# Attention and two feed-forward layers on one core: the stores of the first layer's converted weights in GpSimd's queue in place of SyncE's

## The chip, the cores and the metric

The kernel runs on one core of a Trainium2 chip. The metric is the device time of one execution in microseconds (us). The engines are named as in the profile: PE is TensorE (matmuls), DVE is VectorE, ACT is ScalarE, POOL is GpSimd, and SP is SyncE, which only issues transfers. A "q" behind an engine's name means its instruction queue. Transfers that an engine issues are carried out by the 16 DMA engines of the core.

## The reference

Attention over a band of keys and over block summaries of the keys, then two gated feed-forward layers; 1536 tokens (two batches of 768), 512 wide.

```python
def _attn_ref(q, k, v):                       # (2, 8, 768, 64) each
    k_sum = k.reshape(B, H, nb, 32, D).max(axis=3)
    v_sum = v.reshape(B, H, nb, 32, D).mean(axis=3)
    scores_l = scale * q @ k^T, kept where |i - j| < 16, else -1e9
    scores_s = scale * q @ k_sum^T + log(32)
    a = softmax(concat(scores_l, scores_s))
    return a @ concat(v, v_sum)

def _moe_ref(x, w_gate, w_val, w_out):        # 512 -> 1536 -> 512
    gate = 1.0 / (1.0 + np.exp(-(x @ w_gate)))
    val = x @ w_val
    return (gate * val @ w_out)

def _moe2_ref(x, w1, w2, w3, w_out):          # 512 -> 768 -> 512
    h = np.maximum(np.maximum(x @ w1, x @ w2), x @ w3)
    return (h @ w_out)
```

All inputs are float32. The weights reach the kernel as 64-bit numbers, so each weight tile has to be turned into float32 on the chip.

## The kernel before

**Stages.** Attention is cut into units of a batch, a pair of heads and half a sequence; units of batch 0 come first. As soon as batch 0 is attended, TensorE begins the first layer for it (`make_A`, gate and value products, L791; `make_B`, output products, L830), while the units of batch 1 run in between. From about 228 us on the first layer of batch 1 is computed with fewer, larger products (`make_Q`, L1023, and `make_B` again), then the second layer (`make_P`, L924) and its output (`make_D`, L1124). Each float32 matmul is made of three passes over a high and a low part of both operands, so that a weight tile "w" holds two parts.

**Converting a weight.** `convert` does this for 36 tiles of the first layer (24 of gate and value, "g" and "v", 12 of the output weights, "o", in three groups of 8 + 4). `to_float` loads a 512 KB tile "raw" (L409, SyncE; three buffers) and turns it into float32 in a 256 KB buffer "c" with three VectorE instructions, here called c1 (L416), c2 (L421) and c3 (L425). `split` then writes the high part of "w" on ScalarE (L358) and the low part on VectorE by a subtraction (L361); there are ten "w" buffers. There are only **two "c" buffers**: c1 of a tile can begin when the last but one tile has been split and, if it is a g or v tile, stored.

**Keeping it.** `keep` stores what batch 1 will need again in device memory, directly behind the conversion: a g or v tile is stored from "c" (256 KB, L457, into `kept_g` or `kept_v`), an o tile from "w" (512 KB, L451, into `kept_o`). That is 24 + 12 transfers, all between about 24 and 187 us. They are read back later (L480, L470) by SyncE.

**The order.** Nothing is scheduled on the chip. `Plan.order` sorts all tasks before the kernel is built: each task has an engine, a duration and a due time, and the planner keeps for each engine the time at which it is free, for transfers also a time of the queue. For a transfer of SyncE it reckons with 0.45 us to issue, 0.65 us until it begins and a duration that grows with its size. The instructions of every engine are written in the order that comes out, and each engine works through its own in that order, waiting where data or a buffer is missing. Changed durations in the planner so change the order on all engines. Attention's inputs "k", "q", "v", "vn" (L548), the raw loads and the stores all stand in SyncE's queue.

Of the kernel before, what the change touches and what calls it, by code (L numbers as in the profile page):

```python
# [31 lines left out]
KEEP, AGAIN = 4.0, 6.0  # L32
# [10 lines left out]
SLOW = 1.12  # L43
# [31 lines left out]
class Plan:  # L75
# [11 lines left out]
    def add(self, eng, dur, due, fn, deps=(), new=(), uses=(), after=(), tab=None):  # L87
        t = Task(eng, dur, due, fn, [d for d in deps if d], list(new), list(uses), [d for d in after if d], tab)
        self.tasks.append(t)
        return t  # L90
# [26 lines left out]
    def order(self):  # L117
        engs = ("PE", "DVE", "ACT", "POOL", "SP")
        free = dict.fromkeys(engs, 0.0)
        free["SP"] = 0.6  # L120
        dge = ring = 0.0
        clock = self.Clock()
        free["PE"] = 1.13
        tab = "E"
        taken = {}
        wait, then, ready = {}, {}, {e: [] for e in engs}
        for t in self.tasks:
            pre = t.deps + t.after
            wait[t] = len(pre)
            for d in pre:  # L130
                then.setdefault(d, []).append(t)
            if not pre:
                ready[t.eng].append(t)
        out = []

        def earliest(t):
            at = free[t.eng]
            for d in t.deps:
                at = max(at, d.end + self.lag(d, t) + (t.pad if d.eng != t.eng else 0.0))
            for d in t.after:  # L140
                at = max(at, d.start)
            need = {}
            for b in t.new:
                k = need.get(b.tag, 0)
                need[b.tag] = k + 1
                used = taken.setdefault(b.tag, [])
                i = len(used) + k - b.n
                if i >= 0:
                    for d in used[i].users:
                        if d.end is None:  # L150
                            return None
                        at = max(at, d.end + (0.1 if d.eng != t.eng else 0.0))
            return at

        def pressing(x):
            return x[1].due + (SWITCH if x[1].tab and x[1].tab != tab else 0.0)

        while len(out) < len(self.tasks):
            best = None
            for e in engs:  # L160
                c = [(at, t) for at, t in ((earliest(t), t) for t in ready[e]) if at is not None]
                if not c:
                    continue
                first = min(at for at, _ in c)
                at, t = min((x for x in c if x[0] <= first + SLACK[e]), key=pressing)
                if best is None or at < best[0]:
                    best = at, t
            at, t = best
            ready[t.eng].remove(t)
            t.start = at  # L170
            t.end = at + t.dur
            if t.eng == "PE":
                if t.new and at < FIRST + 5.0:
                    width = min(384, t.new[0].shape[-1] * (t.new[0].shape[1] if len(t.new[0].shape) == 3 else 1))
                    now = free["PE"]
                    while True:
                        end = clock.run(now, width / 2400.0, 1.0, False)
                        if end > at + OVER:
                            break
                        now = clock.run(now, width / 2400.0, 1.0) + 0.001  # L180
                        t.idle += 1
                    at = t.start = max(at, now)
                t.end = clock.run(at, t.dur, t.rows)
            if t.dma:
                dge = max(dge, at) + t.dma
                ring = max(ring, dge + 0.65) + (t.dur * SLOW if t.eng == "SP" else 0.2)
                free[t.eng] = at + t.dur if t.eng != "SP" else dge + 0.025
                t.end = ring
            if t.tab and t.tab != tab:
                tab = t.tab  # L190
                t.end += self.TABLE
            if not t.dma:
                free[t.eng] = t.end
            for b in t.new:
                taken[b.tag].append(b)
            out.append(t)
            for d in then.get(t, ()):
                wait[d] -= 1
                if not wait[d]:
                    ready[d.eng].append(d)  # L200
        return out
# [3 lines left out]
def kernel(  # L205
# [15 lines left out]
    nc = tc.nc  # L221
# [68 lines left out]
    add = plan.add  # L290
# [53 lines left out]
    at = FIRST  # L344
# [42 lines left out]
    def first_use(b, nm, f):  # L387
        if nm == "o" and b:
            return due["B", b, (f // GF, 0), 0, f % GF // 2] + 0.52 * (f % 2)
        if nm == "o":  # L390
            return due["B", b, (f // GF, 0), 0] + 0.52 * (f % GF)
        if nm == "l":
            return due["D", 0, 0, 0] + 0.68 * f
        return due[nm, b, f, 0]
# [3 lines left out]
    def convert():  # L398
# [3 lines left out]
        def to_float(ck, t):  # L402

            nonlocal n
            r = Buf(rp, [128, 2 * 512], I32, "raw", 3)
            c = Buf(cp, [128, 512], I32, "c", 2)

            def load(r=r, ck=ck):
                nc.sync.dma_start(out=r.t, in_=wts[row[ck[1:]]])  # L409

            def half(r, i):
                return r.t.rearrange("p (f two) -> p f two", two=2)[:, :, i]


            def c1(r=r, c=c):
                nc.vector.tensor_scalar(  # L416
                    out=c.t, in0=half(r, 1), scalar1=5, scalar2=2,
                    op0=ALU.logical_shift_left, op1=ALU.logical_shift_right)

            def c2(r=r, c=c):  # L420
                nc.vector.scalar_tensor_tensor(  # L421
                    out=c.t, in0=half(r, 1), scalar=-0x40000000, in1=c.t, op0=ALU.bitwise_and, op1=ALU.bitwise_or)

            def c3(r=r, c=c):
                nc.vector.scalar_tensor_tensor(  # L425
                    out=c.t, in0=half(r, 0), scalar=29, in1=c.t, op0=ALU.logical_shift_right, op1=ALU.bitwise_or)

            n += 1
            l = add("SP", 1.456, WFIRST + WSTEP * n if n <= 8 else t - WLOAD, load, new=[r], after=[prev.get("l")])
            k1 = add("DVE", 0.335, t - 2.7, c1, [l], [c], [r], [prev.get("1")])  # L430
            k2 = add("DVE", 0.602, t - 2.3, c2, [k1], [], [c, r])
            k3 = add("DVE", 0.602, t - 1.6, c3, [k2], [], [c, r])
            prev.update({"l": l, "1": k1})
            return c, k3
# [11 lines left out]
        def keep(ck, t, c, k):  # L446
            nm, f = ck[1:]
            if nm == "o":
                w, k = wt[ck], wready[ck]
                d = kept[nm, f] = Buf(kp, [128, 2, 512], F32, f"kept_o{f}", 1)  # L450
                d.k = add("SP", 1.456, t + KEEP, lambda: nc.sync.dma_start(  # L451
                    out=d.t, in_=w.t.bitcast(F32)), [k], [d], [w])
                return
            if f % 2 == 0:
                kept[nm, f // 2] = Buf(kp, [128, 2, 512], I32, f"kept_{nm}{f // 2}", 1)
            d = kept[nm, f // 2]
            k = add("SP", 0.73, t + KEEP, lambda: nc.sync.dma_start(out=d.t[:, f % 2], in_=c.t),  # L457
                    [k] + ([d.k] if f % 2 else []), [] if f % 2 else [d], [c] + ([d] if f % 2 else []))
            d.k = k

        for ck in chunks:
            t = first_use(*ck) - WREADY
            c, k = to_float(ck, t)
            wt[ck], wready[ck] = split(c, lambda c=c: c.t.bitcast(F32), t, [k])
            keep(ck, t, c, k)
# [9 lines left out]
        for g in range(NG):  # L475
            for nm, j in pairs[GF * g:GF * g + GF]:
                t = due["Q", nm, j, 1] - WREADY
                d = kept[nm, j]
# [9 lines left out]
        for nm, f, b in groups:  # L488
            if b == 0:
                t = due["P", nm, f, 0, 1] - WREADY  # L490
# [3 lines left out]
        for ck in last:  # L494
            t = first_use(*ck) - WREADY
            c, k = to_float(ck, t)
# [747 lines left out]
```

## Time and profile before

| | us |
|---|---|
| three runs, median (lowest to highest) | 551.56 (549.83 to 552.42) |
| the profiled execution | 553.78 |
| its span, first to last instruction | 552.0 |
| TensorE busy (matmuls) | 532.7 |
| VectorE busy | 418.5 |
| ScalarE busy | 305.0 |
| GpSimd busy | 3.7 |

TensorE is the engine with the most work, and it is busy for 96% of the span. The transfers of SyncE's queue take 40.3% of the time of 16 DMA engines, with most of it in the first third. A mean over the span says little here: the stages differ, and the stores that the change touches lie in the first 187 us alone. A row of a timeline gives the start, the duration, the engine, the line and the tile; in brackets stands how long the engine had been idle before it, and what ended that. A wait is put down to what came last. "issue" means that the profile shows nothing that was waited for.

### The profile page before, as it was taken

How to read it: one execution, taken by the hardware profiler on the slowest of the kernel's cores; microseconds unless marked ns; L12 is line 12 of the kernel's file. 1: busy time of each engine (PE TensorE's matmuls, PEld its weight loads, DVE VectorE, ACT ScalarE, POOL GpSimd, SP SyncE). 2: the span in 40 equal slices, each digit the busy share in tenths (PEclk: the TensorE clock that was granted, in tenths of full speed). 3: DMA queues.
4: the chain of work that ended last, by engine and by line, in shares of the span. 5: the costliest groups of instructions: out<-in, count | busy, mean ns of one | idle time of the engine just before them, and what ended most of it. 6: DMA issues, size and time to landing. Idle time of an engine off the chain costs nothing.

```text
span 552.0 us, 10064 instructions
## 1 busy us (share of the span) xinstructions
PE 532.7 (96%) x3805; PEld 506.0 (92%) x3805; DVE 418.5 (76%) x988; ACT 305.0 (55%) x722; POOL 3.7 (1%) x18
## 2 busy tenths in 40 slices
PE   7799999979979999999999999999999999999997
PEld 5688999969979999999999999998999999998886
DVE  3999997588788766998287589999999998995000
ACT  3879879578547785565465166544434343463111
POOL 2000000000000000000000000000000000000000
PEclk9999999999999999999999999999999999999999
DMA  8999897678866510143025028111322223201121
GB/s 270 292 309 319 293 350 222 225 250 290 275 167 185 214 50 2 38 148 121 28 93 173 14 77 300 43 39 43 112 76 78 77 78 113 77 2 39 57 76 58
DMA packets 28128, 78.25 MB, mean 142 GB/s; under 512 B 3504, under 2 KB 6960, under 8 KB 28080
## 3 DMA queue, kind: packets, MB, share of 16 engines
q1 hardware_dynamic: 24960, 73.87, 40.3%
q10 hardware_dynamic: 3120, 3.74, 1.9%
q8 instruction: 30, 0.49, 0.4%
q14 instruction: 18, 0.15, 0.1%
HBM read 61.28 MB, written 15.73 MB: 140 GB/s over the span
## 4 chain that ended last, share of the span: by engine, by line
PE 67%; DMA 13%; DVE 12%; ACT 4%; issue 1%; SPq 1%; ACTq 1%; DVEq 0%
PE m L830 13%; PE m L924 11%; PE s L924 10%; PE m L1124 9%; PE s L1023 8%; PE m L1023 8%; PE m L791 6%; DMA vn<-in_vn_dram 3%; DMA kept_g<-c 3%; DMA k<-in_kn_dram 2%; DMA kept_v<-c 2%; DVE w L361 2%; DVE c L425 2%; DVE c L421 2%; DVE e L661 1%
## 5 line engine op out<-in xcount | busy, mean ns | idle before, releaser
L791 PE MATMUL m<-x,w 128*128 128x384 f32 x576 | 109.6, 341 | 1.6 <-DVE t L813 1.3
L830 PE MATMUL m<-h,w 128*128 128x384 f32 x576 | 105.2, 336 | 0.0
L791 PEld LDWEIGHTS m<-x,w 128*128 128x128 f32 x576 | 98.6, 188 | 4.2 <-DVE t L813 1.6
L830 PEld LDWEIGHTS m<-h,w 128*128 128x128 f32 x576 | 99.6, 188 | 0.5 <-issue 0.3
L924 PE MATMUL m<-x,w 128*128 128x384 f32 x294 | 56.2, 334 | 0.6 <-ACT t L939 0.6
L924 PE MATMUL s<-f,w 128*128 128x384 f32 x294 | 56.0, 334 | 0.0
L358 ACT ACTIVATE w<-c 128x512 fp32r<-128x512 f32 (+1 forms) x60 | 35.5, 597 | 35.0 <-DVE c L425 28.4
L924 PEld LDWEIGHTS m<-x,w 128*128 128x128 f32 x294 | 51.4, 188 | 0.9 <-ACT t L939 0.9
L924 PEld LDWEIGHTS s<-f,w 128*128 128x128 f32 x294 | 51.4, 188 | 0.1
L667 ACT ACTIVATE e<-e,nm 128x120 f32<-128x120 f32 x96 | 36.7, 385 | 20.3 <-DVE nm L661 20.1
L1023 PE MATMUL s<-f,w 128*128 128x384 f32 x252 | 47.9, 335 | 0.0
L1023 PE MATMUL m<-f,w 128*128 128x384 f32 x252 | 46.7, 334 | 0.0
L1023 PEld LDWEIGHTS s<-f,w 128*128 128x128 f32 x252 | 43.9, 188 | 0.6 <-ACT t L1038 0.6
L1023 PEld LDWEIGHTS m<-f,w 128*128 128x128 f32 x252 | 43.9, 188 | 0.1
L421 DVE SCALAR_TENSOR_TENSOR c<-raw,c 128x512 int32<-128x512 int32 x60 | 41.1, 686 | 0.6
L425 DVE SCALAR_TENSOR_TENSOR c<-raw,c 128x512 int32<-128x512 int32 x60 | 41.1, 685 | 0.3
L361 DVE TENSOR_TENSOR w<-c,w 128x512 fp32r<-128x512 f32 (+1 forms) x60 | 38.6, 644 | 2.0 <-ACT w L358 2.0
L361 DVE TENSOR_TENSOR w<-raw,w 128x512 fp32r<-128x512 f32 (+1 forms) x48 | 28.2, 620 | 14.7 <-ACT w L358 14.6
L358 ACT ACTIVATE h<-t 128x384 fp32r<-128x384 f32 x48 | 24.9, 523 | 22.7 <-DVE t L1063 15.3
L416 DVE TENSOR_SCALAR c<-raw 128x512 int32<-128x512 int32 x60 | 25.2, 423 | 13.7 <-DMA kept_v<-c 9.7
L358 ACT ACTIVATE w<-raw 128x512 fp32r<-128x512 f32 (+1 forms) x48 | 25.8, 572 | 14.4 <-PE m L830 11.1
L361 DVE TENSOR_TENSOR h<-t,h 128x384 fp32r<-128x384 f32 x48 | 26.1, 553 | 7.3 <-ACT h L358 7.2
(128 smaller groups left out, 764.7 us busy)
## 6 DMA issues: line engine op xcount, KB each, us to landing
raw<-in_wts_dram SPq DMA_DIRECT2D x60, 512.0 KB, 4.5
kept_o<-w SPq DMA_DIRECT2D x12, 512.0 KB, 4.0
w<-kept_o SPq DMA_DIRECT2D x12, 512.0 KB, 6.5
k<-in_kn_dram SPq DMA_DIRECT2D x8, 400.0 KB, 6.4
q<-in_qt_dram SPq DMA_DIRECT2D x16, 192.0 KB, 5.5
v<-in_vw_dram SPq DMA_DIRECT2D x16, 192.0 KB, 5.1
kept_g<-c SPq DMA_DIRECT2D x12, 256.0 KB, 5.6
kept_v<-c SPq DMA_DIRECT2D x12, 256.0 KB, 4.5
```

The source lines that it names most:

```text
L358: nc.scalar.activation(out=dst, in_=src, func=ACTF.Copy)
L361: nc.vector.tensor_tensor(out=dst, in0=src, in1=h.bitcast(F32), op=ALU.subtract)
L416: nc.vector.tensor_scalar(out=c.t, in0=half(r, 1), scalar1=5, scalar2=2, op0=ALU.logical_shift_left, op1=ALU.logical_shift_right)
L421: nc.vector.scalar_tensor_tensor(out=c.t, in0=half(r, 1), scalar=-0x40000000, in1=c.t, op0=ALU.bitwise_and, op1=ALU.bitwise_or)
L425: nc.vector.scalar_tensor_tensor(out=c.t, in0=half(r, 0), scalar=29, in1=c.t, op0=ALU.logical_shift_right, op1=ALU.bitwise_or)
L661: nc.vector.tensor_tensor_reduce(out=e[h].t[:, t], in0=ps[h].t[:, t], in1=masks[:, var], scale=-SC, scalar=3.0e38, op0=ALU.add, op1=ALU.mi ...
L667: nc.scalar.activation(out=e[h].t[:, t], in_=e[h].t[:, t], func=ACTF.Exp, scale=-1.0, bias=nm.t[:, h, t:t + 1], accum_out=sm.t[:, h, t:t + 1])
L791: nc.tensor.matmul(ps.t, lhsT=w.t.rearrange("p s (k f) -> p s k f", k=KC)[:, wh, kc], rhs=src[kc // 2].t[:, xh, kc % 2], start=(kc == 0 an ...
L830: nc.tensor.matmul(ps.t, lhsT=w.t.rearrange("p s (k f) -> p s k f", k=KC)[:, wh, dm], rhs=h.t[:, xh], start=(i == 0 and j == 0), stop=(i = ...
L924: nc.tensor.matmul(ps.t, lhsT=w.t[:, wh, c:c + 128], rhs=x.t[:, xh, kc], start=new and n == 0, stop=n == 5, skip_group_check=True)
L1023: nc.tensor.matmul(ps.t, lhsT=w.t[:, wh, c:c + 128], rhs=x.t[:, xh, kc], start=new and n == 0, stop=n == 5, skip_group_check=True)
L1124: nc.tensor.matmul(ps.t[:, c0:c1], lhsT=h.t[:, xh, e, c:c + 128], rhs=w.t[:, wh, c0:c1], start=(f == 0 and i == 0), stop=(f == NF2 - 1 and ...
```

## The change

The stores of `keep` are issued by GpSimd, in its own queue, instead of SyncE. The planner gets figures for a transfer of GpSimd: the engine is taken for 1.0 us, the queue begins after 1.65 us, and the transfer ends 1.9 us and 2.2 times its duration after the issue. No instruction of another engine is added or removed; the order of the first 200 us or so changes on PE, DVE, ACT and SP.

```diff
@@ Plan.order
-            if t.dma:
+            if t.dma and t.eng == "POOL":
+                free["POOL"] = at + 1.0
+                ring = max(ring, at + 1.65) + t.dur * SLOW
+                t.end = at + 1.9 + 2.2 * t.dur
+            elif t.dma:
                 dge = max(dge, at) + t.dma
@@ keep
-                d.k = add("SP", 1.456, t + KEEP, lambda: nc.sync.dma_start(
+                d.k = add("POOL", 1.456, t + KEEP, lambda: nc.gpsimd.dma_start(
                     out=d.t, in_=w.t.bitcast(F32)), [k], [d], [w])
+                d.k.dma = 1.0
...
-            k = add("SP", 0.73, t + KEEP, lambda: nc.sync.dma_start(out=d.t[:, f % 2], in_=c.t),
+            k = add("POOL", 0.73, t + KEEP, lambda: nc.gpsimd.dma_start(out=d.t[:, f % 2], in_=c.t),
                     [k] + ([d.k] if f % 2 else []), [] if f % 2 else [d], [c] + ([d] if f % 2 else []))
+            k.dma = 1.0
```

Lines of the kernel after stand four (planner and conversions: L409 is L413, L416 is L420, L421 is L425, L425 is L429, L361 is L365) to six (L548 is L554) further down. In the rows below, the word ahead of "<-" is what is written, the one behind it what is read.

SyncE's queue before, where the second group of weights begins (83 to 96 us):

```order
L409 DMA raw<-in_wts_dram 128x1024
L457 DMA kept_v_1406<-c 128x512
L548 DMA q<-in_qt_dram 128x384
L548 DMA k<-in_kw_dram 128x720 x2
L409 DMA raw<-in_wts_dram 128x1024
L457 DMA kept_g_1360<-c 128x512
L548 DMA v<-in_vw_dram 64x768
L548 DMA v<-in_vw_dram 32x768
L409 DMA raw<-in_wts_dram 128x1024
L457 DMA kept_v_1406<-c 128x512
```

The same place of SyncE's queue after:

```order
L413 DMA raw<-in_wts_dram 128x1024
L554 DMA q<-in_qt_dram 128x384
L554 DMA k<-in_kw_dram 128x720 x2
L413 DMA raw<-in_wts_dram 128x1024 x2
L554 DMA v<-in_vw_dram 64x768
L554 DMA v<-in_vw_dram 32x768
```

and GpSimd's queue after, which holds nothing else there:

```order
L462 DMA kept_g_1331<-c 128x512
L462 DMA kept_v_1362<-c 128x512
L462 DMA kept_g_1331<-c 128x512
L462 DMA kept_v_1362<-c 128x512
L462 DMA kept_g_1546<-c 128x512
```

The stores are gone from between the loads, and each stands behind earlier stores alone.

VectorE before, inside the second group (from the c3 that ended at 102.44 us to the c1 of 112.06 and its c2):

```order
L425 SCALAR_TENSOR_TENSOR c<-raw,c 128x512
L416 TENSOR_SCALAR c<-raw 128x512
L361 TENSOR_TENSOR w<-c,w 128x512
L421 SCALAR_TENSOR_TENSOR c<-raw,c 128x512
L425 SCALAR_TENSOR_TENSOR c<-raw,c 128x512
L416 TENSOR_SCALAR c<-raw 128x512
L361 TENSOR_TENSOR w<-c,w 128x512
L421 SCALAR_TENSOR_TENSOR c<-raw,c 128x512
L425 SCALAR_TENSOR_TENSOR c<-raw,c 128x512
L416 TENSOR_SCALAR c<-raw 128x512
L421 SCALAR_TENSOR_TENSOR c<-raw,c 128x512
```

and VectorE after, one conversion later in the same group:

```order
L429 SCALAR_TENSOR_TENSOR c<-raw,c 128x512
L420 TENSOR_SCALAR c<-raw 128x512
L365 TENSOR_TENSOR w<-c,w 128x512
L425 SCALAR_TENSOR_TENSOR c<-raw,c 128x512
L429 SCALAR_TENSOR_TENSOR c<-raw,c 128x512
L365 TENSOR_TENSOR w<-c,w 128x512
L420 TENSOR_SCALAR c<-raw 128x512
L425 SCALAR_TENSOR_TENSOR c<-raw,c 128x512
L429 SCALAR_TENSOR_TENSOR c<-raw,c 128x512
L420 TENSOR_SCALAR c<-raw 128x512
```

In the first pair of conversions one more subtraction now stands between a c3 and the c1 after the next; otherwise the pattern is the same.

## Rows read from the trace of the kernel before

**Rows 1.** Stages: start:end, length, busy of each engine, PEclk, DMA share, GB/s.

```profile
25.00:50.00 25.00, 24.30 (x355) 22.18 (x354) 23.55 (x85) 21.65 (x76) 0.00 (x0) 1.00 0.95 328
50.00:100.00 50.00, 49.43 (x443) 46.41 (x442) 41.20 (x121) 43.20 (x111) 0.00 (x0) 1.00 0.89 287
100.00:125.00 25.00, 21.38 (x159) 19.19 (x159) 18.86 (x46) 16.04 (x39) 0.00 (x0) 1.00 0.66 216
150.00:175.00 25.00, 22.21 (x167) 20.54 (x166) 20.96 (x64) 13.61 (x47) 0.00 (x0) 1.00 0.64 188
228.00:350.00 122.00, 122.00 (x702) 121.28 (x701) 91.85 (x190) 67.76 (x139) 0.00 (x0) 1.00 0.32 113
```

**Rows 2.** Waits of TensorE, 30 to 230 us: total, times, longest; first two and last.

```profile
PE s L686 <- ACT e L681: 3.1, 2, 1.8
PE s L699 <- issue: 1.5, 1, 1.5
...
PE m L791 <- DVE x L361: 0.3, 1, 0.3
```

**Rows 3.** Timeline of TensorE: start, duration, line, tile; in brackets the idle time before.

```profile
114.96 2.36 PE L791 MATMUL m<-x,w 128*128 128x384 f32 x12 [1.26 <-DVE t L813]
...
119.09 0.90 PE L686 MATMUL s<-ident,e 128*120 128x128 f32 x3 [1.77 <-ACT e L681]
...
155.74 0.90 PE L686 MATMUL s<-ident,e 128*120 128x128 f32 x3 [1.29 <-ACT e L681]
```

**Rows 4.** Timeline of VectorE: two c3, then the c1 that waited.

```profile
90.78 0.69 DVE L425 SCALAR_TENSOR_TENSOR c<-raw,c 128x512 int32<-128x512 int32 x1
...
92.56 0.69 DVE L425 SCALAR_TENSOR_TENSOR c<-raw,c 128x512 int32<-128x512 int32 x1
...
100.09 0.43 DVE L416 TENSOR_SCALAR c<-raw 128x512 int32<-128x512 int32 x1 [2.26 <-issue]
...
104.56 0.43 DVE L416 TENSOR_SCALAR c<-raw 128x512 int32<-128x512 int32 x1 [2.12 <-DMA kept_v<-c]
...
112.06 0.43 DVE L416 TENSOR_SCALAR c<-raw 128x512 int32<-128x512 int32 x1 [2.42 <-DMA kept_v<-c]
...
149.10 0.43 DVE L416 TENSOR_SCALAR c<-raw 128x512 int32<-128x512 int32 x1 [2.44 <-DMA kept_v<-c]
```

**Rows 5.** Waits of VectorE, 0 to 200 us: total, times, longest.

```profile
DVE c L416 <- DMA kept_v<-c: 9.7, 5, 2.4
...
DVE k L636 <- DMA k<-in_kw_dram: 4.3, 4, 1.9
...
DVE c L416 <- issue: 2.3, 1, 2.3
...
DVE c L416 <- DMA kept_g<-c: 1.1, 1, 1.1
```

**Rows 6.** Timeline of SyncE's queue: start and duration of the issue.

```profile
93.77 0.42 SPq L457 DMA_DIRECT2D kept_g<-c  x1
...
95.96 0.50 SPq L457 DMA_DIRECT2D kept_v<-c  x1
...
106.95 0.33 SPq L409 DMA_DIRECT2D raw<-in_wts_dram  x1
107.33 0.42 SPq L457 DMA_DIRECT2D kept_v<-c  x1
```

**Rows 7.** Issue to landing: the 24 stores of L457; ScalarE's stores, KB each, median.

```profile
DMA to landing us min/median/max: 3.4/4.8/7.7
...
out_dram<-c ACTq DMA_DIRECT2D x11, 256.0 KB, 2.0
```

**Rows 8.** Timeline of GpSimd: a longest instruction, and its last one.

```profile
2.59 0.44 POOL L279 TENSOR_SCALAR_AFFINE_SELECT masks<-masks 64x288 f32<-64x288 f32 x1
...
4.75 0.11 POOL L286 MEMSET masks<- 64x16 f32 x1
```

**Rows 9.** Waits of SyncE's queue: total, times, longest.

```profile
SPq L409 <- DVE c L425: 150.7, 34, 23.1
```

## The prediction, made before the changed kernel ran

> **What bounds the kernel now.** I read the profile in this order: the table of stages, for the engine that sets the end; TensorE's waits and its timeline, for the places where that engine stands still; then VectorE's waits and its timeline, for what stands behind those places; and last SyncE's queue and the times to landing, because the change lies there. The stages [rows 1] show TensorE busy for 24.30 of 25 us from 25 us on, and for all of 122 us between 228 and 350. An engine that has work all the time ends when its work is done, so a change in front of it counts only as far as it fills a gap on TensorE or opens one. The gaps that can be filled lie in two stages: 25 − 21.38 = 3.62 us are idle between 100 and 125 us, and 25 − 22.21 = 2.79 us between 150 and 175 us [rows 1]. Over 30 to 230 us the waits of TensorE stand in 7 lines, from 3.1 down to 0.3 us, and sum to 7.7 us [rows 2]. This is all that a better order could win there, 1.4% of the time. A loss has no such limit.
>
> Three of the gaps can be followed back. The matmul group at 114.96 us waited 1.26 us for a VectorE product (L813); the transposes at 119.09 and 155.74 us waited 1.77 and 1.29 us for ScalarE's scaling (L681) [rows 3], which itself needs a VectorE reciprocal. VectorE, in order, stood a short time earlier at c1 (L416), the first step of a conversion, because c1 writes a buffer "c" of which there are only two, and the store of the last but one conversion had not landed: 2.26 us before 100.09, 2.12 before 104.56, 2.42 before 112.06, 2.44 before 149.10 [rows 4]. In the table of waits these are 9.7 us in 5 waits for kept_v, 1.1 in one for kept_g, and one of 2.3 put down to "issue", the one at 100.09 [rows 5]. Its predecessor by two is the store issued at 93.77, so I count it with them: 13.1 us in 7 waits. The stores that are to move are thus what VectorE waits for ahead of three of TensorE's gaps.
>
> **The change part by part.** *Leaving SyncE.* SyncE issues in order, and a store stands behind whatever is in front. The c3 (L425) that started at 90.78 us and took 0.69 ended at 91.47; its store left at 93.77, behind the kw loads and a raw load that the order has in front of it. The next c3 began at 92.56 [rows 4], ended at 93.25, and its store left at 95.96 [rows 6]. From the end of c3 to the c1 that needed the landing, these two took 100.09 − 91.47 = 8.6 us and 104.56 − 93.25 = 11.3 us. In the ordinary case only the raw load that c3 also releases stands ahead: raw at 106.95, store at 107.33 [rows 6], so 0.4 us after c3. With the median of 4.8 us to landing [rows 7] an ordinary store takes 0.4 + 4.8 = **5.2 us from c3's end**.
>
> *Going through GpSimd.* GpSimd has had nothing to do since its last instruction at 4.75 us [rows 8], so its 36 stores wait there for their data alone. The trace shows no transfer that GpSimd issued, so the price is bounded. From below: 2.0 us, a 256 KB store of ScalarE's queue with nothing ahead [rows 7]. From above: 7.7 us, the longest of the stores today [rows 7], if the work of GpSimd costs as much as the worst queue. I take the shortest of today's, 3.4 us [rows 7], which still has one 512 KB raw load in front of it, and add 0.44 us, GpSimd's longest instruction [rows 8]: **3.8 us from c3's end**. It lies nearer to the lower end because the row that is likest, a store behind one load, lies there. The saving is 5.2 − 3.8 = 1.4 us for each ordinary exposed store (bounds +3.2 and −2.5), and 8.6 − 3.8 and 11.3 − 3.8, more than their whole waits, for the two that SyncE held.
>
> *VectorE's waits.* Of the seven, 2.26 and 2.12 go. Of 2.42 and 2.44, 1.02 and 1.04 stay. The other two of kept_v's five are 9.7 − 2.12 − 2.42 − 2.44 = 2.7 us together, 1.4 each, and go, as the 1.1 of kept_g does. So 2.1 of 13.1 us stay.
>
> *TensorE's gaps.* Before 112.06 us VectorE gains 2.26 + 2.12 + 1.4 = 5.8 us, more than the 1.26 + 1.77 that TensorE loses at 114.96 and 119.09; by 149.10 it has gained more still, against 1.29. All three gaps go: **−4.3 us**. What is late next there is TensorE itself. The other 3.4 us of gaps, among them 1.5 of unseen cause [rows 2], stay.
>
> *The planner's new order.* The changed costs give another order up to about 200 us; behind that TensorE's order is the same. In the stretch of shortest cover (second group of weights) both orders put only a c1, one or two subtractions (L361) and c2, c3 between a store and the c1 that needs its buffer: 2.1 us before, 2.1 to 2.7 after. The order therefore hides no more of a store than it did, and part of the 2.1 us that stays on VectorE will be felt. Today 13.1 us of such waits cost 4.3 us on TensorE, 0.33 each; 2.1 × 0.33 = **+0.7 us**.
>
> *Costed at nothing.* SyncE's own freedom: it waits 150.7 us for c3 before raw loads [rows 9], because there are three raw buffers, so the loads come no sooner; VectorE waits for no raw load. Attention's loads no longer stand behind stores; VectorE waited 4.3 us for kw loads [rows 5], and what of that goes adds to 5.8 us that already exceed the gaps. Without that excess it would be worth up to 4.3 × 0.33 = 1.4 us. The 12 kept_o stores hold "w" buffers, of which there are ten, and VectorE and TensorE show no wait for one. The bytes are the same.
>
> Sum: −4.3 + 0.7 = −3.6 us. The profiled execution took 553.78 us, 1.78 more than its span of 552.0; it gives 550.2. The median of the three runs is 551.56, and on that scale the forecast is **548.0 us**, 0.65% less.
>
> **A rule that speaks against it.** In the rows the two stores that SyncE held left 2.3 and 2.7 us late, and that is where the first two waits begin. The Trainium skill, DMA: Bandwidth & Descriptors, section "Issuing engines are not separate DMA queues", says that transfers of all issuing engines end up on the same 16 DMA engines, and that issuing from several engines "will only save the time on the sequencer it takes to initiate the DMA". By that rule the sum would hold only the time lost ahead of the issue, and the trace shows that this is not small here; what it would make of the sum is the first rival.
>
> **The rivals.** *No change.* The store shares the DMA engines with the raw load of the same moment, and the DMA engines are 0.89 to 0.95 busy until 100 us [rows 1]; it lands at 5.2 us after c3 as today. Then only the two held stores gain. For it: landing, not issue, is most of the 5.2 us. Against it: from 100 us on the DMA share is 0.66 [rows 1], there is room. The attention units also go through ScalarE's exponentials, for which VectorE waits too; in this case the 1.77 and 1.29 stay, the 1.26 goes, and the new order returns 0.7: 551.56 − 1.26 + 0.7 = 551.0 us.
>
> *Slower: GpSimd and VectorE in each other's way.* What GpSimd must write for a transfer falls right behind c3, when VectorE is already in its next instructions, a c1 of 0.43 us among them [rows 4]. If the store then lands 7.7 us after c3, each of the seven waits grows by 2.5 us, 17.5 us on VectorE, at 0.33 on TensorE: +5.7, **557.3 us**. It decides against the change from 5.2 us on. For it: VectorE is 23.55 of 25 us busy in the first stage [rows 1]. Against it: a c1 is short beside 3.8 us. The Trainium skill, SBUF — State Buffer, section "SBUF: two separate sides", names such a mechanism: while VectorE runs an instruction in a mode that takes two ports, GpSimd cannot write the descriptors of its transfers. No run here shows it yet.
>
> *All gaps go.* Stores at 2.0 us, no VectorE wait left: 551.56 − 7.7 = 543.9 us.
>
> **How the numbers follow.** About 0.5% (2.8 us) is what a measurement here can tell from no change, so "faster" is below 548.8 and "slower" above 554.3. The forecast gets 0.46; its store lies between 2.0 and 5.2 us, and with it the time between 545 and 551, so that 0.34 falls below 548.8 and 0.12 above. All gaps gone: 0.10. No change: 0.22. Slower: 0.22. This makes faster 0.44, same 0.34, slower 0.22. The range begins at 544.0, the best that the gaps allow, and ends at 555.5, where the slower rival is at two thirds of its price; about 0.15 lie beyond it.
>
> **What would show it.** Right: c1's waits for kept stores fall from 13.1 to under 4 us; stores land 3 to 4.5 us after c3; TensorE is idle under 2 us between 100 and 125 us. Wrong: c1 lasts much longer than 0.43 us, or stores land later than 5.2 us after c3. The forecast also fails if the new order opens a gap on TensorE in a place where there is none today.

## The result, and the profile after

The changed kernel is slower, by little, but its interval lies above 1. Its median is 557.9 us (556.81 to 558.69) beside 551.16 us for the kernel before on the same chip; the ratio is 1.0121, with a 95% interval of 1.0091 to 1.0151. Measured again later it came out at 1.0119 (1.0095 to 1.0142). The prediction of 548.0 us had the wrong sign, and the time lies above its range.

The profiled execution took 558.69 us with a span of 557.0, so 5.0 us more than the 552.0 of before. The stages of after, to be laid beside [rows 1] (start:end, length, busy of PE, PEld, DVE, ACT and POOL, PEclk, DMA share, GB/s):

```profile
25.00:50.00 25.00, 24.05 (x343) 21.55 (x342) 20.33 (x70) 18.42 (x63) 2.70 (x5) 0.93 0.97 325
50.00:100.00 50.00, 48.04 (x426) 45.13 (x425) 44.45 (x129) 37.46 (x106) 4.93 (x9) 0.97 0.82 282
100.00:125.00 25.00, 22.93 (x168) 20.70 (x167) 19.19 (x52) 17.39 (x44) 2.86 (x5) 1.00 0.84 264
125.00:150.00 25.00, 22.79 (x155) 20.75 (x153) 19.65 (x50) 16.66 (x42) 3.42 (x7) 0.93 0.68 245
150.00:175.00 25.00, 25.00 (x219) 23.20 (x219) 17.71 (x59) 14.06 (x46) 2.59 (x5) 1.00 0.65 185
228.00:350.00 122.00, 122.00 (x704) 121.58 (x703) 91.83 (x188) 67.19 (x137) 0.00 (x0) 1.00 0.32 112
```

Two things happened at once. The idle time of TensorE fell where the prediction looked for it: from 3.62 to 2.07 us between 100 and 125 us, and from 2.79 to nothing between 150 and 175. But VectorE, 23.55 us busy between 25 and 50 us before, is busy for 20.33 us there now. Behind 228 us nothing changed.

Idle sums are a poor measure here, since the same matmuls can count as more or less busy time, as the next rows show. A fixed place in the work is better: the first matmul that has the same work ahead of it in both kernels. The first `m<-f,w` of L1023 (L1029 after) is such a place. The work from the start up to it, of before and of after (columns as above):

```profile
0.00:227.38 227.38, 213.46 (x2023) 196.53 (x2024) 177.91 (x518) 162.03 (x448) 3.70 (x18) 1.00 0.69 225
```

```profile
0.00:232.01 232.01, 219.23 (x2023) 201.09 (x2024) 178.45 (x518) 157.55 (x444) 23.55 (x54) 0.97 0.67 221
```

The same 2023 matmuls and 518 VectorE instructions take 4.6 us longer. VectorE's own work is the same, 177.9 and 178.5 us, so it stood still for 4 us more. A second mark is the first matmul of L583 (`s<-vr,avg`; L589 after), with 917 matmuls ahead of it before and 914 after (the source views of the two lines; the first start is the mark):

```profile
L583 PE MATMUL s<-vr,avg x8: 272/272/273, 77.2 to 189.5; 96*128 96x128 f32 x8
```

```profile
L589 PE MATMUL s<-vr,avg x8: 272/273/273, 81.3 to 194.1; 96*128 96x128 f32 x8
```

So 4.1 of the 4.6 us are lost in the first 81 us, in which the prediction had looked for no change. A second profile of the changed kernel (e11 below) has the marks at 80.8 and 232.1 us.

VectorE's timeline shows what stands there. Two c1 of before, the third and the fourth of the kernel:

```profile
30.03 0.43 DVE L416 TENSOR_SCALAR c<-raw 128x512 int32<-128x512 int32 x1 [1.07 <-DMA kept_g<-c]
34.67 0.43 DVE L416 TENSOR_SCALAR c<-raw 128x512 int32<-128x512 int32 x1
```

and the c1 of after, from the third on: the four that waited for a store in the first 60 us, and behind that the two that waited longest:

```profile
25.20 0.42 DVE L420 TENSOR_SCALAR c<-raw 128x512 int32<-128x512 int32 x1
29.93 0.43 DVE L420 TENSOR_SCALAR c<-raw 128x512 int32<-128x512 int32 x1 [0.59 <-DMA kept_v<-c]
...
40.17 0.43 DVE L420 TENSOR_SCALAR c<-raw 128x512 int32<-128x512 int32 x1 [1.17 <-DMA kept_v<-c]
44.48 0.43 DVE L420 TENSOR_SCALAR c<-raw 128x512 int32<-128x512 int32 x1 [0.55 <-DMA kept_g<-c]
49.73 0.43 DVE L420 TENSOR_SCALAR c<-raw 128x512 int32<-128x512 int32 x1 [0.82 <-DMA kept_v<-c]
...
98.22 0.43 DVE L420 TENSOR_SCALAR c<-raw 128x512 int32<-128x512 int32 x1 [2.26 <-issue]
...
140.39 0.43 DVE L420 TENSOR_SCALAR c<-raw 128x512 int32<-128x512 int32 x1 [2.94 <-DMA kept_g<-c]
```

The third and the fourth conversion stand about 5 us earlier, and the next four 1 to 5 us. Before, one c1 waited for a store in the first 60 us; now four do, in a stretch where VectorE had hardly been idle. Over 0 to 205 us the waits for stores have not fallen to under 4 us, as the prediction's sign for being right asked, but risen from the 13.1 us of [rows 5] to 14.5 (VectorE's waits of after: total, times, longest; those put down to "issue" are counted, as in the 13.1):

```profile
DVE c L420 <- issue: 6.0, 3, 2.3
DVE c L420 <- DMA kept_g<-c: 4.3, 3, 2.9
DVE c L420 <- DMA kept_v<-c: 4.2, 5, 1.2
```

What that does to TensorE is seen in its waits between 30 and 235 us, the counterpart of [rows 2]:

```profile
PE s L692 <- ACT e L687: 3.0, 2, 1.6
PE s L692 <- DVE e L682: 2.0, 1, 2.0
PE m L797 <- DVE x L365: 0.9, 1, 0.9
PE m L797 <- DVE t L819: 0.7, 1, 0.7
```

The gaps that the prediction followed back are shorter or gone, but there are others: 2.0 us at 52.42 us and 1.6 at 143.12, where TensorE did not wait before. The sum, 7.1 us with a last wait of 0.5, is nearly the 7.7 of before.

The stores themselves, all 24 from "c" (the view of L462: duration of the issue min/median/max in ns, first and last start; then issue to landing), and one of them in the timeline behind its c3:

```profile
L462 POOL DMA_DIRECT2D kept_g<-c x12: 539/540/699, 17.1 to 161.6; - x12
L462 POOL DMA_DIRECT2D kept_v<-c x12: 539/539/544, 23.7 to 166.6; - x12
...
DMA to landing us min/median/max: 4.5/5.5/7.0
```

```profile
47.34 0.69 DVE L429 SCALAR_TENSOR_TENSOR c<-raw,c 128x512 int32<-128x512 int32 x1
...
48.33 0.54 POOL L462 DMA_DIRECT2D kept_g<-c  x1 [4.04 <-DVE sm L678]
```

GpSimd starts 0.3 us after the end of c3 at 48.03. With the median of 5.5 us to landing a store is in place 5.8 us after its c3, against the 5.2 reckoned for an ordinary store of before, though no load stands ahead of it in its own queue any more. Only earlier stores do, the last of them here issued 4.6 us before.

### The profile page after: what moved, and what is told of

The parts are those of the page before. It is cut to its first block, busy times and chain, and to the rows that moved or that the text cites. A ratio compares the mean times of both kernels' runs of the same rounds, so it can differ in the third digit from the quotient of the medians.

```text
span 557.0 us, 10096 instructions
## 1 busy us (share of the span) xinstructions
PE 538.5 (97%) x3805; PEld 510.7 (92%) x3805; DVE 419.0 (75%) x988; ACT 300.5 (54%) x718; POOL 23.6 (4%) x54
## 4 chain that ended last, share of the span: by engine, by line
PE 71%; issue 11%; DMA 8%; DVE 5%; ACT 2%; POOL 1%; SPq 1%; ACTq 0%; POOLq 0%
PE m L836 14%; PE m L930 11%; PE s L930 10%; PE m L1130 9%; PE s L1029 8%; PE m L1029 8%; PE m L797 8%; DMA kept_g<-c 3%; DMA vn<-in_vn_dram 2%; DMA k<-in_kn_dram 1%; DMA kept_v<-c 1%; PE s L692 1%; PE s L705 1%; DVE x L365 1%; DVE u L877 1%
## 5 line engine op out<-in xcount | busy, mean ns | idle before, releaser
L797 PE MATMUL m<-x,w 128*128 128x384 f32 x576 | 112.8, 348 | 1.6 <-DVE x L365 0.9
L797 PEld LDWEIGHTS m<-x,w 128*128 128x128 f32 x576 | 101.3, 193 | 4.0 <-DVE x L365 1.2
L930 PE MATMUL m<-x,w 128*128 128x384 f32 x294 | 56.2, 335 | 0.6 <-ACT t L945 0.6
L930 PEld LDWEIGHTS m<-x,w 128*128 128x128 f32 x294 | 51.4, 188 | 0.9 <-ACT t L945 0.9
L1029 PE MATMUL s<-f,w 128*128 128x384 f32 x252 | 47.9, 336 | 0.0
L1029 PE MATMUL m<-f,w 128*128 128x384 f32 x252 | 46.7, 335 | 0.0
L1029 PEld LDWEIGHTS s<-f,w 128*128 128x128 f32 x252 | 43.9, 188 | 0.6 <-ACT t L1044 0.6
L1029 PEld LDWEIGHTS m<-f,w 128*128 128x128 f32 x252 | 43.9, 188 | 0.1
L425 DVE SCALAR_TENSOR_TENSOR c<-raw,c 128x512 int32<-128x512 int32 x60 | 41.1, 687 | 0.6
L429 DVE SCALAR_TENSOR_TENSOR c<-raw,c 128x512 int32<-128x512 int32 x60 | 41.0, 686 | 0.5
L365 DVE TENSOR_TENSOR w<-c,w 128x512 fp32r<-128x512 f32 (+1 forms) x60 | 38.7, 646 | 2.2 <-ACT w L362 2.0
L365 DVE TENSOR_TENSOR w<-raw,w 128x512 fp32r<-128x512 f32 (+1 forms) x48 | 28.2, 620 | 15.4 <-ACT w L362 15.4
L420 DVE TENSOR_SCALAR c<-raw 128x512 int32<-128x512 int32 x60 | 25.2, 423 | 16.5 <-issue 6.0
L362 ACT ACTIVATE w<-raw 128x512 fp32r<-128x512 f32 (+1 forms) x48 | 25.7, 572 | 14.4 <-PE m L836 11.1
L365 DVE TENSOR_TENSOR h<-t,h 128x384 fp32r<-128x384 f32 x48 | 26.1, 553 | 7.6 <-ACT h L362 7.6
```

Source lines behind the costliest of these rows:

```text
L362: nc.scalar.activation(out=dst, in_=src, func=ACTF.Copy)
L365: nc.vector.tensor_tensor(out=dst, in0=src, in1=h.bitcast(F32), op=ALU.subtract)
L420: nc.vector.tensor_scalar(out=c.t, in0=half(r, 1), scalar1=5, scalar2=2, op0=ALU.logical_shift_left, op1=ALU.logical_shift_right)
L425: nc.vector.scalar_tensor_tensor(out=c.t, in0=half(r, 1), scalar=-0x40000000, in1=c.t, op0=ALU.bitwise_and, op1=ALU.bitwise_or)
L429: nc.vector.scalar_tensor_tensor(out=c.t, in0=half(r, 0), scalar=29, in1=c.t, op0=ALU.logical_shift_right, op1=ALU.bitwise_or)
L797: nc.tensor.matmul(ps.t, lhsT=w.t.rearrange("p s (k f) -> p s k f", k=KC)[:, wh, kc], rhs=src[kc // 2].t[:, xh, kc % 2], start=(kc == 0 an ...
```

## The experiments

Four explanations were open. **Order**: the new figures for GpSimd's transfers make the planner believe that stores land early, it places c1 too early, and VectorE, in order, blocks what stands behind. **Queue**: GpSimd's stores are late in themselves. **GpSimd and VectorE**: they hinder each other. **Clock**: TensorE's granted clock is 0.93 in four of the first six stretches of 25 us after, 1.00 in all of before, and the loss is matmuls at half speed. The traces speak against the third: the view of L420 gives c1 a median of 426 ns (401 to 433) after, that of L416 422 (404 to 429) before, no issue on GpSimd took longer than 0.70 us, and no store longer than 7.0 us to land. So does e1, in which GpSimd issues the stores and the kernel is faster.

All ratios are to the kernel before on the same chip, with 95% intervals.

| run | what it is | median us | ratio | interval |
|---|---|---|---|---|
| e1 | order before, stores by GpSimd | 549.51 | 0.9953 | 0.9931–0.9975 |
| e2 | order after, stores by SyncE | 562.99 | 1.0179 | 1.0143–1.0215 |
| e3 | after, third "c" | 544.25 | 0.9855 | 0.9824–0.9885 |
| e4 | before, third "c" | 543.41 | 0.9836 | 0.9807–0.9866 |
| e5 | after, planner's figure 5.6 us | 548.32 | 0.9939 | 0.9917–0.9961 |
| e6 | e1, third "c" | 543.94 | 0.9857 | 0.9834–0.9879 |
| e7 | after, two gaps filled | 558.47 | 1.0124 | 1.0100–1.0149 |
| e8 | e5, third "c" known to the planner | 544.97 | 0.9877 | 0.9855–0.9899 |
| e9 | after, planner's figure 1.5 us | 557.50 | 1.0104 | 1.0074–1.0133 |
| e10 | after, planner's figure 7.6 us | 546.26 | 0.9892 | 0.9867–0.9917 |
| e11 | after, once more | 558.66 | 1.0119 | 1.0095–1.0142 |
| e12 | before, stores planned 2 us later | 543.74 | 0.9842 | 0.9820–0.9865 |

Some came out beside what was expected. e1 and e12 are faster than all that was named for them, e2 is slower, and e4 is faster by 3.6 us than the 547 us that the prediction's term for the gaps gave. e8 fell between its two cases. e5's waits for stores at c1 in the first 60 us came to 1.8 us, not to under 1.

### The queue and the order, each alone

The change has two halves that can be parted, since the planner's engine is only a name. In e1 the planner goes on taking the stores for SyncE's, so that the order is that of before on every engine, and GpSimd issues them:

```diff
-    d.k = add("SP", 1.456, t + KEEP, lambda: nc.sync.dma_start(
+    d.k = add("SP", 1.456, t + KEEP, lambda: nc.gpsimd.dma_start(
...
-    k = add("SP", 0.73, t + KEEP, lambda: nc.sync.dma_start(out=d.t[:, f % 2], in_=c.t),
+    k = add("SP", 0.73, t + KEEP, lambda: nc.gpsimd.dma_start(out=d.t[:, f % 2], in_=c.t),
```

> Every engine's instructions in the order of the kernel before; only the 36 stores are issued by GpSimd. Theory A (the new order costs the time: it puts the conversions 2 to 5 us earlier into VectorE's queue in the first 60 us): about 551 to 552 us. Theory B (the stores themselves cost it, since they land about 5.6 us after c3 in place of 5.2, and share the DMA engines with attention's loads): 555 to 558 us. If both have a part, between.

e2 is the other half: the diff of the change as it stands, with `nc.sync` left in both places.

> Every engine's instructions in the order of the kernel after; the 36 stores are issued by SyncE at the place that the new order gives them. Theory A (the order): 556 to 558 us, with TensorE gaps near 52 and 143 us as in the kernel after. Theory B (the stores in GpSimd's queue): about 551 us.

The queue alone gains 0.5%, the order alone loses 1.8%, about 10 us. The product, 0.9953 × 1.0179 = 1.0131, lies inside the interval of the whole change: the two halves simply add. The loss is the order's and not the queue's. In e1 the waits of 1.26 and 1.77 us of [rows 3] at 114.96 and 119.09 are gone, as predicted, and the stretch from 100 to 125 us is nearly full:

```profile
100.00:125.00 25.00, 24.59 (x201) 22.53 (x203) 19.76 (x48) 16.89 (x41) 2.85 (x5) 1.00 0.67 207
```

In e2 the damage of the order stands bare. VectorE's timeline, then TensorE's:

```profile
29.38 0.43 DVE L420 TENSOR_SCALAR c<-raw 128x512 int32<-128x512 int32 x1 [4.01 <-DMA kept_g<-c]
...
56.00 0.43 DVE L420 TENSOR_SCALAR c<-raw 128x512 int32<-128x512 int32 x1 [5.22 <-DMA kept_v<-c]
```

```profile
34.42 1.55 PE L705 MATMUL s<-at,v 120*64 120x64 f32 x24 [3.17 <-ACT vs L592]
...
58.69 0.87 PE L692 MATMUL s<-ident,e 128*120 128x128 f32 x3 [5.41 <-DVE e L682]
```

The two gaps on TensorE, 8.6 us, end 5.0 and 2.7 us after the two waits on VectorE, 9.2 us, and all lie in the first 60 us. The first matmul of L589 comes at 88.3 us here, 11.1 later than before, and the first of L1029 at 237.78, 10.4 later. One instruction count does differ between the orders: ScalarE runs 722 instructions in the order of before (e1 too) and 718 in that of after (e2 too), since four of 22 table loads (ACT_TABLE_LOAD) fall away. That is in the new order's favour.

### Taking away what c1 waits for

If the order costs only because c1 waits for stores, a third buffer "c" must make the orders equal. Every third of the 36 tiles gets its buffer from memory that attention's pool has left; the order stays as it is.

```diff
+        if self.tag == "c" and Buf.turn < 36:
+            Buf.turn += 1
+            if Buf.turn % 3 == 0:
+                self.t = Buf.third.tile(self.shape, self.dtype, tag="cx", name="cx", bufs=1)
+                return
...
+    Buf.turn, Buf.third = 0, ap_
```

> The kernel after with a third c buffer for the 36 tiles of the first layer (taken from attention's memory), in the same order, so that c1 has no store to wait for. If c1's waits (14.5 us on VectorE, 8 of them put down to kept stores and 3 to issue) are what the change costs: 551 us or less, and no half-speed stretch near 52 us. If the time is lost by the shared DMA engines or by the order as such: 555 us or more.

> The kernel before with the same third c buffer, in its own order. By the prediction's term for the gaps (13.1 us of waits on VectorE cost 4.3 us on TensorE): about 547 us. If TensorE's gaps hang on attention's chain through ScalarE instead: 550 to 551 us, although c1 no longer waits.

> The order of the kernel before, stores issued by GpSimd, and the third c buffer. If the queue's gain of 0.5% consists of waits at c1: no gain over the third buffer alone (0.9836), so 543 to 544 us. If it consists of SyncE's loads going out sooner: another 0.3 to 0.5%, 541 us.

With the third buffer all three lie between 0.9836 and 0.9857, with intervals that overlap. The order's 1.8% is gone, and so is the queue's 0.5%. In their profiles no c1 waits for a store, apart from one of 0.5 us in e4 (VectorE's waits at c1, e3 and then e4):

```profile
DVE c L426 <- DMA raw<-in_wts_dram: 1.3, 3, 0.7
```

```profile
DVE c L422 <- DMA raw<-in_wts_dram: 0.7, 1, 0.7
DVE c L422 <- DMA kept_g<-c: 0.5, 1, 0.5
```

Both halves of the change thus act through the waits at c1 and through nothing else that can be measured here. The two marks tell where, in us of one profile each:

| order, issued by | first mark, with third "c" | second mark, with third "c" |
|---|---|---|
| before, SyncE (before, e4) | 77.2, 75.4 | 227.4, 216.9 |
| before, GpSimd (e1, e6) | 78.5, 76.4 | 225.4, 218.5 |
| after, GpSimd (after, e3) | 81.3, 77.0 | 232.0, 219.1 |

The waits at c1 cost the kernel before 10.5 us in all, 1.8 of them ahead of the first mark, and the changed kernel 12.9, with 4.3 ahead of it. Beside e1, which has the same queue, the new order loses 6.6 us: 2.8 in the first stretch and 3.8 behind it.

The prediction's quotation from the Trainium skill, DMA: Bandwidth & Descriptors, section "Issuing engines are not separate DMA queues", fits: where nothing waits for the store, its issue from another engine gained nothing (e6 against e4), and where VectorE waits, the gain was 0.5% (e1). That this 0.5% is the time saved ahead of the issue is my reading.

### The clock

Twelve and ten matmuls whose results nothing reads are put in front of the transposes at 52.4 and 143.1 us:

```diff
             t1.pad = PAD if b else 0.0
+            t1.fill = {(5, 1): 12, (11, 0): 10}.get((i, h), 0)
...
-                for _ in range(t.idle):
+                for _ in range(t.idle + t.fill):
```

> The kernel after with 12 and 10 matmuls that nothing reads, put ahead of the two transposes at 52.4 and 143.1 us, where TensorE waited 1.96 and 1.60 us and then ran at half its clock. If the lower clock is a cost of its own: granted clock 1.00 from 50 to 75 and from 125 to 150 us, and 1 to 3 us less than the kernel after, 555 to 557 us. If it only falls where TensorE would have waited anyway: 557 to 558 us.

The filling did what it was to do. The group behind the first gap, of after and of e7, in TensorE's timeline:

```profile
52.94 3.12 PE L797 MATMUL m<-x,w 128*128 128x384 f32 x9
```

```profile
52.84 1.83 PE L798 MATMUL m<-x,w 128*128 128x384 f32 x9
```

Both stretches now have a granted clock of 1.00 (e7, columns as above), and the time is that of after:

```profile
50.00:75.00 25.00, 25.00 (x264) 22.38 (x265) 24.58 (x68) 21.22 (x58) 2.15 (x4) 1.00 0.82 268
...
125.00:150.00 25.00, 24.10 (x192) 20.96 (x190) 19.68 (x50) 16.74 (x43) 3.85 (x7) 1.00 0.67 236
```

```profile
139.80 0.43 DVE L420 TENSOR_SCALAR c<-raw 128x512 int32<-128x512 int32 x1 [3.29 <-DMA kept_g<-c]
...
162.01 0.90 PE L692 MATMUL s<-ident,e 128*120 128x128 f32 x3 [1.87 <-ACT e L687]
```

VectorE's c1 stood a little sooner and waited longer, 3.29 in place of 2.94 us, and TensorE has a new gap at 162.01: I read this as arriving sooner at the next wait. In the first 25 us, which the filling does not reach, the clock was lower still (0.80). e9 (below) closes that hole: its profile has 0.93 there and 1.00 from 25 us on, and it is as slow as after, while e10 has 0.80 in the first 25 us and is fast. The lower clock is a sign of the gaps, not the loss.

### The planner's figure

For a 256 KB store (duration 0.73) the change's formula gives 1.9 + 2.2 × 0.73 = 3.5 us from issue to landing, and it counts no load that is under way. It is the one figure changed in three runs, with 1.5, 5.6 and 7.6 us (0.8, 4.9 and 6.9 in the line):

```diff
-                t.end = at + 1.9 + 2.2 * t.dur
+                t.end = at + 4.9 + 1.0 * t.dur
```

> The kernel after with the planner's figure for the end of a 256 KB store at 1.5 us in place of 3.5 (measured: 5.6). If the time follows how far the figure lies below the measured landing: as slow as the kernel after or slower, 557 to 562 us. If the kernel after was only an unlucky order: anywhere from 547 to 560 us.

> The kernel after, unchanged, beside the two others on the same chip: 1.009 to 1.015 of the kernel before, as in its first timing.

> The kernel after with one figure of the planner changed: a store of GpSimd ends 4.9 us and once its duration after the issue (5.6 us for 256 KB, as measured in the kernel after) in place of 1.9 us and 2.2 times its duration (3.5 us). Theory C (the planner takes the stores for 2 us too quick and so puts c1 too early into VectorE's order, where it blocks attention): VectorE's waits at c1 in the first 60 us go from 3.1 us to under 1, and the time falls to 547 to 551 us. Rival (the order of the kernel before was good by chance and any new one costs about 1.8%): 555 us or more.

> The kernel after with the same figure at 7.6 us, 2 us above the measured landing. If only a figure that is too low harms, because c1 then blocks VectorE: 546 to 551 us, near the run with 5.6 us. If the right figure itself matters on both sides: 552 us or more, since conversions then come late for TensorE.

With 1.5 us the ratio is 1.0104, with 3.5 us 1.0121 and 1.0119, with 5.6 us 0.9939, with 7.6 us 0.9892. The step lies between 3.5 and 5.6, and the measured landing, 5.5 us, lies there too; 1.5 and 3.5 give nearly the same order. The waits of c1 for stores, with those put down to "issue", are 13.8 us, 14.5, 7.4 and 1.2 in the four profiles. With 7.6 us this one is left:

```profile
DVE c L420 <- DMA kept_v<-c: 1.2, 1, 1.2
```

VectorE's timelines show what the figure does to the order. Between a c3 and the c1 after the next, which needs the landing of that c3's store, stands other work of VectorE, and only this work hides the store. For the fourth to the eighth conversion it sums to 4.0 to 5.8 us with 1.5 and with 3.5, to 5.8 to 6.4 with 5.6, and to 8.1 to 8.5 with 7.6, and a store takes 5.8 us from its c3. In the order of before two of these five are as short (5.3 and 3.9, and behind the 3.9 e1 waits 2.1 us); the others have 7.6 to 9.4. Each figure gives one order, so the sizes are those of four orders and not a law; the sign is plain.

e8 has e5's figure, and the planner knows of the third buffer:

> The measured price of the stores in the planner and a third c buffer of which the planner knows, stores issued by GpSimd. If all that was lost were waits at c1: 541 to 544 us, as with the third buffer in the old order. If a new order carries a loss of its own: 546 us or more.

At 0.9877 it is no better than the third buffer in an order that was not made for it (e3, e4, e6).

### Without GpSimd

If the figure is what counts, SyncE's stores should gain from an honest one too. e12 is the kernel before, in which the planner takes the 36 stores to land 2.0 us later than it did; no instruction is added, moved to another engine or given another buffer.

```diff
-                t.end = ring
+                t.end = ring + t.late
...
+                d.k.late = 2.0
...
+            k.late = 2.0
```

> The kernel before (stores issued by SyncE), with 2 us added in the planner to the end of each of the 36 stores, so that its order follows. If the gain of the runs with a higher figure comes from the order, whoever issues: 545 to 549 us, c1's waits on VectorE down from 13.1 to under 5 us. If it needs GpSimd's queue, because in SyncE's the stores hold the loads or the loads the stores: 550 us or more.

The ratio is 0.9842 (0.9820 to 0.9865): 8 us faster than the kernel before and, by the two ratios, about 15 faster than the change. VectorE's waits for stores fall from 13.1 us to 4.6 (0 to 205 us), and the stages fill (stages of e12; the last row goes to the first matmul of its L1025):

```profile
DVE c L416 <- DMA kept_v<-c: 2.8, 3, 1.1
DVE c L416 <- DMA kept_g<-c: 1.8, 3, 1.1
```

```profile
25.00:50.00 25.00, 25.00 (x410) 22.54 (x411) 24.52 (x92) 23.80 (x84) 0.00 (x0) 1.00 0.95 322
...
100.00:125.00 25.00, 25.00 (x221) 23.76 (x221) 21.65 (x62) 19.70 (x51) 0.00 (x0) 1.00 0.74 225
```

```profile
0.00:217.42 217.42, 210.64 (x2023) 195.73 (x2024) 177.87 (x518) 157.71 (x444) 3.70 (x18) 1.00 0.71 236
```

The same 2023 matmuls and 518 VectorE instructions are done 10.0 us sooner than before. The counts within one row are no measure of it: TensorE gets through 410 matmuls between 25 and 50 us, where [rows 1] has 355, but nearly all that come in addition are small ones (24 more each of 64x96 and of 64x24).

## Why the prediction was wrong, step by step

**What bounds the kernel.** Right as a chain: stores hold c1, c1 holds VectorE, VectorE holds TensorE. The third buffer, which takes away the first link, gains 1.6% (e4). Wrong as a measure: "This is all that a better order could win there", 7.7 us of visible gaps. e12 reached the second mark 10.0 us sooner, e4 10.5. Of e12's 10.0 us, 7.1 are idle time ahead of the mark; the rest is busy time. With the clock at 1.00 in both, the same matmuls are 213.46 us busy before and 210.64 in e12, so busy rows can hold time that an order wins back.

**The planner's new order, "+0.7 us".** This step failed, and the sign with it. Alone it costs 1.8%, some 10 us (e2). The prediction compared the cover, the work that stands between a store and the c1 that needs its buffer, only in "the stretch of shortest cover (second group of weights)" and priced what was left at 0.33 us for each us of VectorE. In the first group the new order leaves 4.0 to 5.8 us of cover for the fourth to the eighth conversion, no more than the 5.8 that a store takes. The early start itself is not the fault: e5 begins the third conversion at 24.72 us, after at 25.20, and e5 is faster than the kernel before. Four waits in that stretch come to 3.1 us where 1.1 stood before, and 4.1 us are lost by the mark at 81 us; in e2 10.2 us of waits stand beside 11.1 lost. The price of 0.33 was wrong as well: it set 13.1 us of waits against three visible gaps, and without these waits (e4) the second mark comes 10.5 us sooner, 0.8 for each us; in the first stretch it is 1 or more. That it is so high there because VectorE is full and cannot catch up is my reading. That the loss sits in this stretch is read from the two marks in the traces, too; no run changed the order there alone. It holds wholly for SyncE's queue (e2). With GpSimd's, beside e1, 3.8 of 6.6 us are lost behind 81 us, where the prediction had compared the cover; why the waits at c1 there, 11.3 us beside 11.2, cost more in the new order stays open.

**Going through GpSimd, "3.8 us from c3's end".** Too low: 5.8. It lay inside the bounds given, 2.0 and 7.7, but the value was chosen near the shortest store of SyncE, 3.4 us, while the shortest of GpSimd's took 4.5. The 5.2 us for SyncE's stores is less sure than it looks, too: the trace gives a landing for 14 of the 24 [rows 7]. The planner made the same error with 3.5 us, so the change and its forecast leaned on the same false figure.

**VectorE's waits, 13.1 to 2.1 us.** They rose to 14.5. With the order kept (e1: 4.6 of issue, 4.4 of kept_v, 2.6 of kept_g, and 1.8 put down to VectorE's own c3) they hardly fell either. So what e1 won is not in their sum; that it came from where they stood is a reading.

**TensorE's gaps, −4.3 us.** Right in direction, too large. The queue alone is worth 0.5%, 2.6 us by e1's ratio. The gaps of 1.26 and 1.77 us went in e1; a wait of 1.23 us at 153.66 stayed in the place of the third.

**Costed at nothing.** GpSimd is free indeed, with 0.54 us an issue. SyncE's freedom gave nothing that can be measured: with c1's waits gone, e6 is no faster than e4.

**The rivals.** "Slower" gave 557.3 us, close to the 557.9 measured, and for a wrong reason. Its mechanism, GpSimd and VectorE in each other's way, is not in the trace: c1 takes 426 ns against 422, and the stores land 5.8 us after c3, not 7.7. So the closeness is luck. The Trainium skill, SBUF — State Buffer, section "SBUF: two separate sides", describes such an obstruction; no run here shows it. The prediction had named the real cause only in its last sentence, a new gap on TensorE "in a place where there is none today", without a price. The signs it listed did point the right way once seen: waits not under 4 us, landing later than 5.2 us after c3, a gap at 52.42 us. One bound does not come out of the sum: a store of 2.0 us leaves −4.3 us, so 547.3, and not the 545 that the chances begin at.

## What to carry to other kernels

When a change alters a figure that a planner uses, the new order is a change of its own, and often the larger one: part the two (this order with that queue, that order with this queue) before either is credited. In an in-order engine a step that is placed too early blocks all that stands behind it. So see how much work hides each transfer that a step waits for, and let the planner reckon with landings at or above the measured median, above all where the engine is full; here 2 us more on 36 stores were worth 1.6% without touching an instruction. Compare kernels at a fixed place in the work, not by idle sums.

## What the runs showed of the chip that was not expected

- A 256 KB store from GpSimd, with only stores in its queue, takes 5.5 us from issue to landing (4.5 to 7.0), and SyncE's take 4.8 (3.4 to 7.7) [rows 7] with loads ahead of them, by the 14 of 24 whose landing the trace gives. In the order of before GpSimd's took 5.3 (3.3 to 6.7, e1). The share of the DMA engines was 0.97 between 25 and 50 us.
- GpSimd's issue takes 0.54 us and begins 0.3 us after c3; VectorE's c1 lasts as long as before.
- TensorE's granted clock, a mean of the levels of 1.2 and 2.4 GHz, was 0.93 in stretches with a wait of 1.6 or 2.0 us, and nine matmuls behind one of these took 3.12 us in place of 1.83. Giving the full clock back in two such stretches won nothing (e7): the waits behind them grew.
